# Values of two units in one run: an attention and ELU feed-forward kernel on one core

## The chip, the cores and the metric

The kernel runs on one core of one Trainium2 chip. The metric is the device time of one execution in microseconds (us), the median of three runs. A core has five engines with an instruction stream each: TensorE (PE in the rows, its weight loads PEld), VectorE (DVE), ScalarE (ACT), GpSimd (POOL) and SyncE (SP, which here only issues transfers). They run side by side and wait for each other by semaphores.

## The reference

```python
block, window = (32, 16)
k_sum = k.reshape(B, H, nb, block, D).max(axis=3)
v_sum = v.reshape(B, H, nb, block, D).mean(axis=3)
scores_l = scale * np.matmul(q, k.transpose(0, 1, 3, 2))
mask_l = np.abs(pos[:, None] - pos[None, :]) < window
scores_s = scale * np.einsum('bhsd,bhnd->bhsn', q, k_sum)
scores_s = scores_s + np.log(block)
scores_l_m = np.where(mask_l, scores_l, -1000000000.0)
scores_all = np.concatenate([scores_l_m, scores_s], axis=-1)
...
a = a / (np.sum(a, axis=-1, keepdims=True) + 1e-09)
v_all = np.concatenate([v, v_sum], axis=2)
return np.matmul(a, v_all).astype(np.float32)
...
h = x @ w_in
g = np.where(h > 0.0, h, alpha * (np.exp(np.minimum(h, 0.0)) - 1.0))
return (g @ w_out).astype(np.float32)
```

There are 4 batches, 8 heads, 768 positions and a head dimension of 64. Each query attends to a window of 31 positions and to 24 block summaries. The attention's output, 3072 tokens of 512, goes through a layer of 2048 with ELU and back to 512. All is float32.

## The kernel before

The tokens are cut into six chunks of 512 (`CH`), and a chunk's feed-forward into 16 steps, one for each 128 of the 2048 inner columns. A step is called n, from 0 to 95, with chunk c = n // 16. In each step TensorE does `layer1` (twelve matmuls into `h`, four pieces of x by three products: the float32 values are split into a rounded part and a rest, `xh` and `xl`, `gh` and `gl`, and two parts of each weight) and `layer2` of the step before (twelve matmuls into four accumulators `o`). Between the two, ScalarE takes the exponential of `h`, VectorE makes the ELU of it, ScalarE rounds it to `gh`, and GpSimd subtracts to `gl` (`exp_of`, `elu`, `split`).

The attention that makes the x of the next chunk is spread over the same steps. Its work is in units: a unit is 256 queries (a third of a batch's positions) of one pair of heads, p = 0 to 3. The prologue makes the x of chunk 0; 40 units follow, and eight of them fill a chunk. Unit u has its transposes in step 2u and its values in step 2u + 1, both at the end of the step, in `slot_b`. Its scores come in the even step before, in `slot_a`, between the layers. There too the transfers of the unit after are issued (`load_unit`: `qbd`, `kw`, `vw`, the last two with extra pieces at the edges of a batch). Between scores and transposes, VectorE takes the row maximum (`lowest`), ScalarE the exponentials, GpSimd the normalization. `values` multiplies the transposed weights `pt` with the unit's values `vw[p]` into the bank `o_ps`: eight matmuls by two halves of 64 output partitions, which the profile shows as sixteen. `take_x` brings `o_ps` into x: ScalarE's cast to `xh` (L169), and VectorE's subtraction to `xl` (L170).

Eight banks of PSUM hold four accumulators `o`, two `h`, and two, `a0` and `a1`, that scores, transposes, means and values take in turn after the first chunk (`bank`). There are four `kw` and `vw` tiles, one for each p, so unit u + 4 writes over those of unit u.

For steps 16 to 95 the order on TensorE and SP is the program's; the order on the other engines comes from a scheduler. SP takes its transfers in order, and one that waits holds up all behind it. Early in the chunks before a new batch (steps 24 to 29 and 48 to 53), further transfers `n` bring keys and values for that batch's summaries, and VectorE reduces them (L439).

Of the kernel before, what the change touches and what calls it, by code (L numbers as in the profile page):

```python
# [17 lines left out]
F32 = mybir.dt.float32  # L18
# [8 lines left out]
P = 128  # L27
# [5 lines left out]
UW = 4  # L33
UT = UW * QW
# [4 lines left out]
def attn_elu_ffn(ctx: ExitStack, tc: tile.TileContext, qT, kT, vT, v, w_in, w_out, out):  # L39
# [19 lines left out]
    att = ctx.enter_context(tc.tile_pool(name="att", bufs=2))  # L59
    ffn = ctx.enter_context(tc.tile_pool(name="ffn", bufs=2))  # L60
    wts = ctx.enter_context(tc.tile_pool(name="wts", bufs=1))
    psum = ctx.enter_context(tc.tile_pool(name="psum", bufs=1, space=bass.MemoryType.PSUM))
# [4 lines left out]
    vw = [const.tile([P, UW, P], F32, name=f"vw{p}") for p in range(NP)]  # L67
# [78 lines left out]
    def transposes(sm, tag, bufs=1):  # L146
        t_ps = psum.tile([P, UW, P], F32, tag=tag, name="t_ps", bufs=bufs)
        for t in range(UW):
            nc.tensor.transpose(t_ps[0:KC, t, :], sm[:, t, :], ident)  # L149
        return t_ps  # L150

    def values(v_t, w0, pt, tag):
        o_ps = psum.tile([P, UT], F32, tag=tag, name="o_ps")
        for t in range(UW):
            for h in range(2):
                nc.tensor.matmul(o_ps[h * D:(h + 1) * D, t * QW:(t + 1) * QW],  # L156
                                 v_t[0:KC, w0 + t, h * D:(h + 1) * D], pt[0:KC, t, h * QW:(h + 1) * QW],
                                 start=True, stop=True)
        return o_ps
# [3 lines left out]
    def new_x(c):  # L163
        xs[c] = (att.tile([P, NP, CH], F32R, tag="xh", name="xh"), att.tile([P, NP, CH], F32R, tag="xl", name="xl"))

    def take_x(o_ps, third, p):
        xh, xl = xs[third // 2]
        cols = slice(third % 2 * UT, (third % 2 + 1) * UT)
        nc.scalar.copy(out=xh[:, p, cols], in_=o_ps)  # L169
        nc.vector.tensor_tensor(out=xl[:, p, cols], in0=o_ps, in1=xh[:, p, cols].bitcast(F32), op=ALU.subtract)  # L170
# [17 lines left out]
    def first_units():  # L188
# [118 lines left out]
        def vals(p, th):  # L307
            take_x(values(v_t[p], th * UW, pts[p][:, th], ("a0", "o0", "o1", "o2")[2 * (p % 2) + th]), th, p)
# [82 lines left out]
    units = [(third, p) for third in range(2, NTH * B) for p in range(NP)]  # L391
# [51 lines left out]
    def bank(c):  # L443

        if c == 0:
            return "a0"
        banks["n"] += 1
        return f"a{banks['n'] % 2}"
# [8 lines left out]
    s_of, sm_of, z_of, pt_of = {}, {}, {}, {}  # L457
# [16 lines left out]

    def unit_transposes(u, c):
        t_ps = transposes(sm_of.pop(u), bank(c))
        pt_of[u] = att.tile([P, UW, P], F32, tag="pt", name="pt", bufs=1)
        return lambda: nc.scalar.copy(out=pt_of[u][0:KC], in_=t_ps[0:KC])

    def unit_values(u, c):  # L480
        third, p = units[u]
        if third % 2 == 0 and p == 0:
            new_x(third // 2)
        o_ps = values(vw[p], 0, pt_of.pop(u), bank(c))
        return lambda: take_x(o_ps, third, p)


    gs = {}
# [85 lines left out]
                put_means(b, p, vw[p])  # L574

    def slot_b(n, c):
        u, odd = divmod(n, 2)
        return (unit_values if odd else unit_transposes)(u, c) if u < len(units) else lambda: None

    def begin_next():  # L580

# [8 lines left out]
    with tc.manual_schedule(engines=set(engines.values())):  # L590
# [7 lines left out]
        for n in range(NF):  # L598
            u, odd = divmod(n, 2)
# [30 lines left out]
            if n > 0:  # L630
                layer2(0, n - 1)
            late, this = this, ahead
            evacuate = slot_b(n, 0)
        list(late)
        split(0, NF - 1, e)
# [3 lines left out]
    with tc.manual_schedule(engines={engines["PE"], engines["SP"]}):  # L639
        for n in range(NF, NCH * NF):  # L640
            c, f = divmod(n, NF)
            u, odd = divmod(n, 2)
            h_ps = layer1(c, f)
            e = exp_of(h_ps)
            turn = elu(e, h_ps)
            split(c, f, e)
            slot_a(n, c)
            if not odd and u + 1 < len(units):
                unit_exps(u + 1, unit_low(u + 1))
                unit_norm(u + 1)  # L650
            for b, first in first_of.items():
                p = n - (2 * first - 8)
                if p == 0:
                    new_summaries(b)
                for q, src in ((p, kT), (p - 2, vT)):
                    if 0 <= q < NP:
                        got = load_summary(b, q, src)
                        with tc.issue_after(turn):
                            summary(b, q, src, got)
            layer2(*divmod(n - 1, NF))  # L660
            slot_b(n, c)()
        layer2(NCH - 1, NF - 1)
# [37 lines left out]
```

## Time and profile before

| | |
|---|---|
| median of 3 runs | 657.42 us (657.16 to 658.16) |
| the profiled execution | 658.07 us |
| its span, from the first to the last instruction | 656.3 us |
| TensorE busy | 639.7 us, 97% of the span |
| ScalarE, VectorE, GpSimd busy | 42%, 40%, 37% |
| granted TensorE clock, mean | 0.99 of full speed |

The profile is one execution; its own time lies within the three runs. Busy times of TensorE are of instructions that overlap, so how long something holds TensorE is read as the difference of two starts.

### The profile page before, as it was taken

Reading aid. Unit: us, or ns where it says so; the run is one execution under the profiler, and the core shown is the slowest. Engines: PE = TensorE matmul, PEld = TensorE weight load, DVE = VectorE, ACT = ScalarE, POOL = GpSimd, SP = SyncE. Lnnn points to the kernel's source line nnn. Section 1 sums busy time; section 2 is a strip of 40 time slices with the busy share of each in tenths; the row PEclk is TensorE's granted clock in tenths of the full one; section 3 lists DMA queues with packets and bytes.
Section 4 is the critical chain, followed back from the end, with each engine's and each line's share of the span. In section 5 each row is a group of like instructions: output and inputs, shape, how many; then the busy total and the mean of one; then the engine's idle time right before and its main releaser. Section 6 shows DMA issues by size and latency. Waiting matters only on the chain.

```text
span 656.3 us, 10774 instructions
## 1 busy us (share of the span) xinstructions
PE 639.7 (97%) x3916; PEld 523.8 (80%) x3916; DVE 265.7 (40%) x856; ACT 275.6 (42%) x750; POOL 245.3 (37%) x263
## 2 busy tenths in 40 slices
PE   8859999999999999999999999999999999999997
PEld 7648878888888878888888888888888888888885
DVE  7868887633224533322233543222322231322222
ACT  6757667644334333343344333433443343322222
POOL 5768989843222322232223232322232222222221
PEclk9969999999999999999999999999999999999999
DMA  9999965114122514121112551211321100100001
GB/s 315 208 317 351 308 212 167 33 36 125 32 56 80 151 34 134 36 60 38 32 35 72 171 137 38 70 32 33 97 64 31 32 1 1 64 1 1 0 1 64
DMA packets 86324, 60.24 MB, mean 92 GB/s; under 512 B 46464, under 2 KB 78464, under 8 KB 86272
## 3 DMA queue, kind: packets, MB, share of 16 engines
q1 hardware_dynamic: 82960, 53.66, 29.4%
q10 hardware_dynamic: 3312, 5.90, 2.4%
q8 instruction: 31, 0.51, 0.3%
q14 instruction: 21, 0.17, 0.1%
HBM read 52.46 MB, written 6.29 MB: 90 GB/s over the span
## 4 chain that ended last, share of the span: by engine, by line
PE 94%; DMA 2%; DVE 2%; ACT 1%; POOL 0%; SPq 0%; issue 0%; DVEq 0%
PE h L499 41%; PE o L527 40%; PE s L463 5%; PE o_ps L156 4%; PE t_ps L149 3%; DMA v<-in_v_dram 1%; DMA raw_w<-in_w_in_dram 1%; DMA raw_w<-in_w_out_dram 1%; DVE sm L130 1%; PE idle L227 1%; ACT sm L137 0%; PE s L290 0%; DVE sh L110 0%; DVE cv L113 0%; POOL raw_w L103 0%; DVE ks L276 0%
## 5 line engine op out<-in xcount | busy, mean ns | idle before, releaser
L499 PE MATMUL h<-xh,w 128*128 128x512 f32 x768 | 262.8, 403 | 0.0
L517 POOL TENSOR_TENSOR gl<-e,gh 128x512 fp32r<-128x512 f32 x96 | 123.9, 1290 | 205.3 <-issue 109.6
L527 PE MATMUL o<-w,gh 128*128 128x512 f32 x768 | 196.4, 394 | 0.0
L499 PEld LDWEIGHTS h<-xh,w 128*128 128x128 f32 x768 | 145.3, 189 | 31.2
L527 PEld LDWEIGHTS o<-w,gh 128*128 128x128 f32 x768 | 141.2, 188 | 28.2 <-issue 0.6
L499 PE MATMUL h<-xl,w 128*128 128x512 f32 x384 | 150.9, 393 | 0.0
L509 DVE TENSOR_SCALAR e<-e 128x512 f32<-128x512 f32 x96 | 45.1, 469 | 254.2 <-ACT e L505 254.1
L505 ACT ACTIVATE e<-h 128x512 f32<-128x512 f32 x96 | 57.4, 598 | 210.9 <-PE h L499 210.0
L144 POOL TENSOR_TENSOR sm<-sm,z 128x480 f32<-128x480 f32 x48 | 47.5, 990 | 157.0 <-ACT gh L516 130.9
L527 PE MATMUL o<-w,gl 128*128 128x512 f32 x384 | 105.3, 389 | 0.0
L516 ACT CAST gh<-e 128x512 fp32r<-128x512 f32 x96 | 59.0, 615 | 72.9 <-DVE e L510 71.6
L137 ACT ACTIVATE sm<-sm,mx 128x120 f32<-128x120 f32 x192 | 73.5, 385 | 26.5 <-DVE mx L130 26.5
L527 PEld LDWEIGHTS o<-w,gl 128*128 128x128 f32 x384 | 72.0, 188 | 15.2 <-POOL gl L517 0.2
L499 PEld LDWEIGHTS h<-xl,w 128*128 128x128 f32 x384 | 72.9, 190 | 13.0
L510 DVE SCALAR_TENSOR_TENSOR e<-h,e 128x512 f32<-128x512 f32 x96 | 66.2, 690 | 2.2
L170 DVE TENSOR_TENSOR xl<-o_ps,xh 128x256 fp32r<-128x256 f32 x48 | 20.0, 423 | 61.4 <-ACT xh L169 61.4
L118 POOL TENSOR_TENSOR w<-cv,w 128x512 fp32r<-128x512 f32 x32 | 42.4, 1325 | 6.7 <-ACT w L117 5.8
L463 PEld LDWEIGHTS s<-kw,qbd 128*128 128x128 f32 x320 | 41.8, 191 | 3.7 <-DVE xl L170 0.7
L130 DVE CUSTOM_DVE_ANT_0 sm<-s,mask 128x120 f32<-128x120 f32 x192 | 42.2, 277 | 1.8 <-PE s L463 1.7
L463 PE MATMUL s<-kw,qbd 128*128 128x120 f32 x320 | 41.9, 274 | 0.6 <-DVE xl L170 0.6
L149 PE MATMUL t_ps<-ident,sm 128*120 128x128 f32 x192 | 29.3, 276 | 8.5 <-DVE mx L130 6.8
L137 ACT ACTIVATION_READ_ACCUMULATOR sm<-sm,mx 128x1 f32 x192 | 36.1, 188 | 0.0
(66 smaller groups left out, 361.1 us busy)
## 6 DMA issues: line engine op xcount, KB each, us to landing
raw_w<-in_w_in_dram SPq DMA_DIRECT2D x16, 512.0 KB, 6.3
raw_w<-in_w_out_dram SPq DMA_DIRECT2D x16, 512.0 KB, 6.1
qbd<-in_qT_dram SPq DMA_DIRECT2D x80, 64.0 KB, 2.3
out_dram<-ot ACTq DMA_DIRECT2D x20, 256.0 KB, 3.8
kw<-in_kT_dram SPq DMA_DIRECT2D x28, 144.0 KB, 5.9
vw<-in_v_dram SPq DMA_DIRECT2D x28, 144.0 KB, 2.9
n<-in_kT_dram SPq DMA_DIRECT2D x16, 192.0 KB, 2.5
n<-in_vT_dram SPq DMA_DIRECT2D x16, 192.0 KB, 2.6
```

Of the source, the lines that this page charges most:

```text
L130: nc.vector.tensor_tensor_reduce(out=sm[:, t, :], in0=s_ps[:, t, :], in1=m, scale=-scale, scalar=3.0e38, op0=ALU.add, op1=ALU.min, accum_o ...
L137: nc.scalar.activation(out=sm[:, t, :], in_=sm[:, t, :], func=AF.Exp, bias=mx[:, t, :], scale=-1.0, accum_out=z[:, t, :])
L144: nc.gpsimd.tensor_tensor(out=sm, in0=sm, in1=z.broadcast_to([P, UW, KC]), op=ALU.mult)
L149: nc.tensor.transpose(t_ps[0:KC, t, :], sm[:, t, :], ident)
L463: nc.tensor.matmul(s_of[u][:, t, :], qbd[u % 2][:, t, :], kw[p][:, t, :], start=True, stop=True)
L499: nc.tensor.matmul(h_ps, w[:, a, cols], bb[:, cc, :], start=(k == 0), stop=(k == 3 * NCC - 1))
L505: nc.scalar.activation(out=e, in_=h_ps, func=AF.Exp)
L509: nc.vector.tensor_scalar(out=e, in0=e, scalar1=1.0, scalar2=-1.0, op0=ALU.min, op1=ALU.add)
L510: top = nc.vector.scalar_tensor_tensor(out=e, in0=h_ps, scalar=0.0, in1=e, op0=ALU.max, op1=ALU.add)
L516: nc.scalar.copy(out=gh, in_=e)
L517: nc.gpsimd.tensor_tensor(out=gl, in0=e, in1=gh.bitcast(F32), op=ALU.subtract)
L527: nc.tensor.matmul(o_acc[c][s], a[:, s * P:(s + 1) * P], w[:, bb, :], start=first and f == 0, stop=last and f == NF - 1)
```

## The change

Beyond the first chunk (c > 0), a unit's values no longer stand at the end of each odd step. In steps with n % 4 == 1 nothing stands there. In steps with n % 4 == 3 the values of two units, p and p + 1 of the same third, are written behind each other into the two halves of one bank, and then both are taken into x. The transposed weights have two buffers in place of one, since two units' now wait at a time.

```diff
-    def values(v_t, w0, pt, tag):
-        o_ps = psum.tile([P, UT], F32, tag=tag, name="o_ps")
+    def values(v_t, w0, pt, tag=None, o_ps=None):
+        if o_ps is None:
+            o_ps = psum.tile([P, UT], F32, tag=tag, name="o_ps")
...
         t_ps = transposes(sm_of.pop(u), bank(c))
-        pt_of[u] = att.tile([P, UW, P], F32, tag="pt", name="pt", bufs=1)
+        pt_of[u] = att.tile([P, UW, P], F32, tag="pt", name="pt")
         return lambda: nc.scalar.copy(out=pt_of[u][0:KC], in_=t_ps[0:KC])
...
+    def values_of_two(u, c):
+
+        third, p = units[u]
+        if third % 2 == 0 and p == 0:
+            new_x(third // 2)
+        o_ps = psum.tile([P, 2, UT], F32, tag=bank(c), name="o_ps")
+        for i in range(2):
+            values(vw[p + i], 0, pt_of.pop(u + i), o_ps=o_ps[:, i, :])
+        for i in range(2):
+            take_x(o_ps[:, i, :], third, p + i)
+        return lambda: None
...
     def slot_b(n, c):
+
         u, odd = divmod(n, 2)
-        return (unit_values if odd else unit_transposes)(u, c) if u < len(units) else lambda: None
+        if u >= len(units) or (c > 0 and n % 4 == 1):
+            return lambda: None
+        if not odd:
+            return unit_transposes(u, c)
+        return unit_values(u, c) if c == 0 else values_of_two(u - 1, c)
```

The line numbers of the changed kernel are one to eighteen higher. In its order rows a name like `vw_76` is a tile with its number: `vw_76` to `vw_79` are those of p = 0 to 3.

**TensorE, the ends of steps 17 and 19.** The order at the end of step 17 before:

```order
L527 MATMUL o_1989<-w_0_699,gl 128x512
L527 MATMUL o_1990<-w_0_699,gl 128x512
L527 MATMUL o_1991<-w_0_699,gl 128x512
L527 MATMUL o_1992<-w_0_699,gl 128x512
L156 MATMUL o_ps<-pt,vw_76 64x64 x8
L499 MATMUL h<-xh,w_2_730 128x512
L499 MATMUL h<-xl,w_2_730 128x512
```

and now:

```order
L540 MATMUL o_1989<-w_0_699,gl 128x512
L540 MATMUL o_1990<-w_0_699,gl 128x512
L540 MATMUL o_1991<-w_0_699,gl 128x512
L540 MATMUL o_1992<-w_0_699,gl 128x512
L512 MATMUL h<-xh,w_2_730 128x512
L512 MATMUL h<-xl,w_2_730 128x512
```

Layer 2 is followed by layer 1 of step 18 with nothing between. The end of step 19 now, with the semaphores that each instruction waits for:

```order
L540 MATMUL o_1991<-w_2_850,gl 128x512
L540 MATMUL o_1992<-w_2_850,gl 128x512
L157 MATMUL o_ps<-pt,vw_76 64x64 [waits DVE_49]
L157 MATMUL o_ps<-pt,vw_76 64x64 x7
L157 MATMUL o_ps<-pt,vw_77 64x64 [waits DMAHW2_49,Activation_49]
L157 MATMUL o_ps<-pt,vw_77 64x64 x7
L512 MATMUL h<-xh,w_4_882 128x512 [waits DVE_49]
```

Unit 8's values stand behind unit 9's transposes now, directly ahead of unit 9's values. For comparison, the last values of the prologue, which the change does not touch; five units' worth of them stand behind each other (`values` is called once for each third), and these are the last four:

```order
L156 MATMUL o_ps<-pt_509,v_90 64x64 [waits DMAHW1_49]
L156 MATMUL o_ps<-pt_509,v_90 64x64
L156 MATMUL o_ps<-pt_509,v_90 64x64 [waits DMAHW0_49]
L156 MATMUL o_ps<-pt_509,v_90 64x64 x5
L156 MATMUL o_ps<-pt_509,v_90 64x64 [waits DVE_49]
L156 MATMUL o_ps<-pt_509,v_90 64x64 x7
L156 MATMUL o_ps<-pt_549,v_91 64x64 [waits DMAHW3_49,DVE_49,Pool_49]
L156 MATMUL o_ps<-pt_549,v_91 64x64
L156 MATMUL o_ps<-pt_549,v_91 64x64 [waits DMAHW2_49]
L156 MATMUL o_ps<-pt_549,v_91 64x64 x5
L156 MATMUL o_ps<-pt_549,v_91 64x64 [waits DVE_49]
L156 MATMUL o_ps<-pt_549,v_91 64x64 x7
```

There, too, instructions in the middle of a row of values wait for transfers and engines.

**ScalarE, the casts of units 8 and 9.** Before, around the end of step 19:

```order
L505 ACTIVATE e<-h 128x512 [waits PE_49,Pool_49]
L516 CAST gh<-e 128x512 [waits DVE_49]
L169 CAST xh<-o_ps 128x256 [waits PE_49]
L505 ACTIVATE e<-h 128x512 [waits PE_49,Pool_49]
L137 ACTIVATE sm,z<-sm,mx 128x120 [waits DVE_49] x4
```

and now:

```order
L518 ACTIVATE e<-h 128x512 [waits PE_49,Pool_49]
L529 CAST gh<-e 128x512 [waits DVE_49]
L170 CAST xh<-o_ps 128x256 [waits PE_49]
L170 CAST xh<-o_ps 128x256 [waits DVE_49]
L518 ACTIVATE e<-h 128x512 [waits PE_49,Pool_49]
L137 ACTIVATE sm,z<-sm,mx 128x120 [waits DVE_49] x4
```

The cast of unit 8 has moved from step 17 to here, and the second cast waits for VectorE. On VectorE the two subtractions have moved in the same way.

**SP, the transfers of unit 14, issued for step 24.** Before:

```order
L398 DMA qbd_70<-in_qT_dram 64x4x64 [waits DMAHW3_49,PE_49]
L398 DMA qbd_70<-in_qT_dram 64x4x64 [waits DMAHW4_49]
L404 DMA kw_74<-in_kT_dram 128x3x96 [waits DMAHW5_49]
L408 DMA vw_78<-in_v_dram 96x3x128 [waits DMAHW6_49]
L416 DMA kw_74<-in_kT_dram 128x80 [waits DMAHW7_49]
L417 DMA vw_78<-in_v_dram 80x128 [waits DMAHW0_49]
L430 DMA n<-in_kT_dram 128x384 [waits DVE_49,DMAHW1_49,Activation_49,Pool_49]
```

and now:

```order
L399 DMA qbd_70<-in_qT_dram 64x4x64 [waits DMAHW3_49,PE_49]
L399 DMA qbd_70<-in_qT_dram 64x4x64 [waits DMAHW4_49]
L405 DMA kw_74<-in_kT_dram 128x3x96 [waits DMAHW5_49]
L409 DMA vw_78<-in_v_dram 96x3x128 [waits DMAHW6_49,PE_49]
L417 DMA kw_74<-in_kT_dram 128x80 [waits DMAHW7_49]
L418 DMA vw_78<-in_v_dram 80x128 [waits DMAHW0_49,PE_49]
L431 DMA n<-in_kT_dram 128x384 [waits DVE_49,DMAHW1_49,Activation_49,Pool_49]
```

The order of SP's transfers is the same all through the program. What is new is that the `vw` transfers of units with p = 0 and 2 wait for TensorE; those with p = 1 and 3 do not.

## Rows read from the trace of the kernel before

**Rows 1.** The page, part 1: busy us, share of the span, instructions.

```profile
PE 639.7 (97%) x3916; PEld 523.8 (80%) x3916; DVE 265.7 (40%) x856; ACT 275.6 (42%) x750; POOL 245.3 (37%) x263
```

**Rows 2.** The page, part 4: the chain that ended last, by engine.

```profile
PE 94%; DMA 2%; DVE 2%; ACT 1%; POOL 0%; SPq 0%; issue 0%; DVEq 0%
```

**Rows 3.** What TensorE waited for from 31 us on: total, times, longest.

```profile
PE t_ps L149 <- DVE mx L130: 6.8, 1, 6.8
```

**Rows 4.** Timeline of TensorE, step 84, without attention: start, us, what.

```profile
583.13 0.39 PE L499 MATMUL h<-xh,w 128*128 128x512 f32 x1
...
585.86 1.98 PE L527 MATMUL o<-w,gh 128*128 128x512 f32 x8
...
588.58 0.39 PE L499 MATMUL h<-xh,w 128*128 128x512 f32 x1
```

**Rows 5.** Timeline of TensorE, steps 41 and 42.

```profile
306.52 0.48 PE L499 MATMUL h<-xh,w 128*128 128x512 f32 x1
...
309.36 1.98 PE L527 MATMUL o<-w,gh 128*128 128x512 f32 x8
...
312.17 0.69 PE L156 MATMUL o_ps<-pt,vw 120*64 120x64 f32 x16
312.79 0.50 PE L499 MATMUL h<-xh,w 128*128 128x512 f32 x1
...
315.64 1.05 PE L463 MATMUL s<-kw,qbd 128*128 128x120 f32 x8
316.45 2.07 PE L527 MATMUL o<-w,gh 128*128 128x512 f32 x8
318.36 1.07 PE L527 MATMUL o<-w,gl 128*128 128x512 f32 x4
```

**Rows 6.** Timeline of TensorE, values in the prologue.

```profile
24.01 0.69 PE L156 MATMUL o_ps<-pt,v 120*64 120x64 f32 x16 [0.58 <-POOL v L174]
...
25.67 2.55 PE L156 MATMUL o_ps<-pt,v 120*64 120x64 f32 x80
```

**Rows 7.** Windows: busy us by engine, granted clock (PEclk), DMA share, GB/s.

```profile
25.60:28.30 2.70, 2.62 (x82) 2.42 (x80) 1.32 (x3) 1.88 (x5) 2.02 (x3) 1.00 0.77 230
306.52:319.62 13.10, 13.10 (x80) 10.77 (x78) 3.73 (x15) 4.92 (x14) 3.53 (x4) 1.00 0.17 40
```

**Rows 8.** Timeline of ScalarE, VectorE and TensorE at the start of step 32.

```profile
247.45 0.37 ACT L169 CAST xh<-o_ps 128x256 fp32r<-128x256 f32 x1 [1.43 <-PE o_ps L156]
250.45 0.60 ACT L505 ACTIVATE e<-h 128x512 f32<-128x512 f32 x1 [2.62 <-PE h L499]
...
247.86 0.42 DVE L170 TENSOR_TENSOR xl<-o_ps,xh 128x256 fp32r<-128x256 f32 x1 [2.49 <-ACT xh L169]
...
249.06 0.39 PE L499 MATMUL h<-xl,w 128*128 128x512 f32 x1
...
249.74 0.39 PE L499 MATMUL h<-xl,w 128*128 128x512 f32 x1
```

**Rows 9.** Timeline of ScalarE and GpSimd, from h to gl of step 41.

```profile
309.62 0.60 ACT L505 ACTIVATE e<-h 128x512 f32<-128x512 f32 x1 [2.17 <-PE h L499]
311.44 0.62 ACT L516 CAST gh<-e 128x512 fp32r<-128x512 f32 x1 [1.22 <-DVE e L510]
...
312.19 1.28 POOL L517 TENSOR_TENSOR gl<-e,gh 128x512 fp32r<-128x512 f32 x1 [3.65 <-issue]
```

**Rows 10.** SP, TensorE, VectorE near step 24; last row: all transfers n.

```profile
187.29 0.48 SPq L408 DMA_DIRECT2D vw<-in_v_dram  x1
...
188.93 12.32 SPq L430 DMA_DIRECT2D n<-in_kT_dram  x4
...
194.39 0.50 PE L499 MATMUL h<-xh,w 128*128 128x512 f32 x1
...
199.88 1.00 DVE L439 TENSOR_REDUCE ks<-n 128x12 f32<-128x384 f32 x2
...
DMA to landing us min/median/max: 2.3/2.5/2.7
```

## The prediction

> **What bounds the kernel now.** I read the page first. TensorE is busy for 639.7 us, 97% of the span, no other engine for more than 42% of the span [rows 1], and the chain that ended last lies on TensorE for 94% [rows 2]. Because a busy TensorE need not be one that runs at its pace, I then read what it waits for: from 31 us to the end the waits view has a single wait of TensorE, 6.8 us in the first chunk's first step [rows 3], which the change does not touch. So from step 16 on nothing feeds TensorE late, and a time there can only come from what TensorE itself executes and from how its instructions follow each other. That is read from starts in the timeline, not from busy sums, since matmuls overlap.
>
> A step without attention is the yardstick: layer 1 starts at 583.13, layer 2 at 585.86, the next step's layer 1 at 588.58 [rows 4]. Each layer's twelve matmuls take 2.72 us, a step 5.44. Against that stands step 41, an odd step with values, and the layer 1 of step 42 after it [rows 5]. Layer 2 runs from 309.36 to the first values matmul at 312.17, 2.81 us instead of 2.72. The values stand from 312.17 to the next layer 1 at 312.79, 0.62. That layer 1 runs to the scores at 315.64, 2.85 instead of 2.72. So one run of values costs 0.09 + 0.62 + 0.13 = 0.84 us of TensorE, of which some 0.2 is a slower entry and a slower first matmul after it. The same pattern stands in all 32 odd steps from 17 to 79. (The layer 1 of step 41, 2.84, pays 0.12 for the transposes ahead of it. That stays.)
>
> **What the change takes away and adds on TensorE.** Units 8 to 39 come after the first chunk: 16 pairs. Each pair had two runs, and now has one, in the steps with n % 4 == 3. As the order rows show, the steps with n % 4 == 1 go from layer 2's last matmul straight to layer 1. The instruction count is the same: sixteen profiled matmuls for a unit.
>
> Taken away for each pair: one run, 0.84 us.
>
> Added: the second unit's sixteen matmuls, directly behind the first's. The prologue has exactly this. A single unit there is 16 matmuls in 0.69 us, and five units back to back are 80 in 2.55 [rows 6], so each further unit costs (2.55 - 0.69)/4 = 0.465 us, 29 ns a matmul, 58 ns for a pair of halves, at the same granted clock of 1.00 as the steps have [rows 7]. Those five write four banks in turn, read three pt tiles, and carry semaphore waits in the middle of the run, as their order rows show; at 0.465 a unit, waits that are long met cost nothing. The new run has the same kind of wait at its second unit.
>
> The bounds of this term: 0.465 is also the pace within one run, and nothing in the rows is faster, so it is the lower end. The upper end is 0.62, a whole run with its start and its end again, if the other half of the bank or the wait breaks the stream [rows 5]. I take 0.465, since [rows 6] shows the same instructions back to back.
>
> What the trace shows of the pace is 29 ns a matmul [rows 6]. The Trainium skill's "TensorE: Matmul & The Clock Gate" (section "Wait — 56ns, not 53.3ns?") speaks against the change: with hardware decode off it gives about 62 ns per matmul as the bound for small matmuls. By that figure sixteen more would be an estimated 0.99 us, more than the 0.84 taken away, and the sum would be some 2.4 us slower. The trace does not agree that this bound holds here.
>
> Sum: (0.84 - 0.465) x 16 = 0.375 x 16 = **6.0 us**; with the upper bound (0.84 - 0.62) x 16 = 3.5 us.
>
> **What moves beside TensorE, and what hides it.**
>
> *Taking the values out of the bank.* Both units share a bank, so no cast starts before the whole run is done, and by the order rows of ScalarE the second cast waits for VectorE, that is for the first subtraction: cast, subtraction, cast, subtraction, one after the other. Behind the waiting cast on ScalarE stands the exp of the next h. It matters first where the next step reads that x, the four chunk edges (into steps 32, 48, 64 and 80). At step 32 today the cast runs from 247.45 for 0.37 us and the subtraction from 247.86 for 0.42 [rows 8], 0.87 from a cast's start to the next free start with the 0.04 between them. So the first xl is ready at 248.28 and the second at 249.15. Layer 1 takes pair 2's xl in its eighth matmul at 249.06 and pair 3's in its eleventh at 249.74 [rows 8]: margins of 0.78 and 0.59 us, and exp waits until 250.45 anyway. Nothing is on the path. If the cover were gone, each us late would cost a us at only four places. In steps 27 and 51 a subtraction stands behind a summary reduce that waits for its transfer; that holds the pair up by the reduce, and only there.
>
> *A shorter way to layer 2.* With its values gone, step 41 gives its h less time until layer 2 needs gh and gl. Today exp starts at 309.62, gh is done at 312.06 and gl at 313.47 [rows 9]. They are needed at 316.45 and 318.36 [rows 5], and after the change 0.84 earlier, 315.61 and 317.52. Margins of 3.5 and 4.0 us remain. The steps without attention have even less time between and do not wait [rows 3, 4].
>
> *The values' transfers.* By the order rows the vw loads of even units (vw_76, vw_78) now also wait for TensorE: the unit that used the tile before has its values two steps later, at the end of step n - 1 for the load issued by step n. Behind that wait, in SP's order, stand the rest of the load and in steps 24 and 48 the first summary transfers, which VectorE takes in its own order. For step 24 the vw load was issued at 187.29, the first n at 188.93, 1.64 later [rows 10]. Now vw goes when the values of step 23 end, no later than the start of step 24 at 194.39. So the first n goes at 196.0 and lands 2.5 later, at 198.5, its second half some half a us behind; VectorE reduces the first at 199.88 [rows 10]. Margin about 1.3 us; were it gone, VectorE would be late by that much, with the 3.5 us of the paragraph above before TensorE feels it. What else is behind the wait, the edge pieces of kw and vw of a unit, is first needed by the scores two steps later, over 12 us by the steps' lengths [rows 5]. SP's next qbd load waits for scores of the coming step anyway.
>
> *The rest.* The second pt buffer only removes a wait. Nothing of the prologue, the first chunk or the last sixteen steps changes.
>
> The profiled execution took 658.07 us, 0.65 above the median of the runs, 657.42. Its sum gives 658.07 - 6.0 = 652.1. I carry the difference over to the median: **651.4 us**, 0.9% faster. A change below 0.2%, 1.3 us, cannot be told from none here.
>
> **The rivals.**
>
> *The second unit pays for a run of its own* (0.62 for 0.465). For it: the run now crosses to another half of one bank and to a tile that ScalarE wrote a step ago, which the prologue's runs do not have in this form. Against it: the unbroken 80 matmuls [rows 6]. 657.42 - 3.5 = 653.9.
>
> *The time comes back as a wait*: a chunk edge, VectorE in the twelve summary steps, or a late transfer takes what the steps gave. Against it are the margins of 0.59, 1.3 and 3.5 us; to eat 6 us at four edges, 1.5 at each, the last xl would have to be 2.1 us later than worked out. 657.4.
>
> *The halves fall apart, slower than before*: a unit's two matmuls of 64 columns run beside each other today, 58 ns for both. If, in the run of two, each took 58 ns by itself, the second unit would cost 16 x 0.058 = 0.93 against 0.84 taken away: 16 x 0.09 = 1.4 us slower, 658.9. It decides from 0.84/16 = 52 ns a matmul on. Against it: 29 ns over 80 matmuls [rows 6]. The figure of the Trainium skill's page on TensorE, told above, would do its harm at this place.
>
> **How the numbers follow.** My forecast has 0.83, the second unit with a run of its own 0.08, the wait that comes back 0.05, slower 0.04. The likeliest alone would be 650.7 to 652.2: 0.02 us of reading error on a pair's 0.375 is 0.3 us, and the three runs shown lie within 1.0. The range takes in the second case: 650.6 to 653.9, and leaves out the two last. Faster by over 0.2%: 0.83 + 0.08 = 0.91; same 0.05; slower 0.04.
>
> **What would show it.** In the changed kernel's timeline: steps with n % 4 == 1 of 6.27 - 0.09 - 0.62 = 5.56 us (6.27 from 306.52 to 312.79 in [rows 5]); the layer 1 behind them at 2.72; a run of 32 values matmuls that holds from its start to the next layer 1 for 0.62 + 0.465 = 1.08; the step around it 6.73. No wait of TensorE after the first chunk. Cast, subtraction, cast, subtraction at each pair, and SP waiting for TensorE ahead of vw of even units. I would be wrong if the run of two shows a hole in its middle, if layer 1 at steps 32, 48, 64 or 80 shows idle time ahead of an xl matmul, or if layer 2 of an odd step starts late.

## The result: 0.9% faster, and the profile after

The changed kernel takes 652.14 us (median of four runs, 650.75 to 653.99), the kernel before in the same set 657.79 (657.16 to 658.33): a ratio of 0.9908 [0.9891, 0.9925]. Put on the 657.42 from which the prediction started, that is 651.4 us. That this meets the forecast to the tenth is luck: two further sets, below, give 652.5 and 650.6 on the same base. The two medians lie 5.65 us apart; the sum gave 6.0. Either is several times what this measurement can tell from no change, 1.3 us.

**The steps.** First the timeline of the changed kernel on TensorE, from step 41 to the scores of step 44 (start, us, what). Its first rows stand against [rows 5].

```profile
306.03 0.48 PE L512 MATMUL h<-xh,w 128*128 128x512 f32 x1
...
308.87 1.98 PE L540 MATMUL o<-w,gh 128*128 128x512 f32 x8
...
311.59 0.39 PE L512 MATMUL h<-xh,w 128*128 128x512 f32 x1
...
314.31 1.05 PE L464 MATMUL s<-kw,qbd 128*128 128x120 f32 x8
...
318.29 0.47 PE L512 MATMUL h<-xh,w 128*128 128x512 f32 x1
...
321.12 1.98 PE L540 MATMUL o<-w,gh 128*128 128x512 f32 x8
...
323.93 1.15 PE L157 MATMUL o_ps<-pt,vw 120*64 120x64 f32 x32
325.01 0.50 PE L512 MATMUL h<-xh,w 128*128 128x512 f32 x1
...
327.86 1.05 PE L464 MATMUL s<-kw,qbd 128*128 128x120 f32 x8
```

Step 41 is 5.56 us (306.03 to 311.59) and has layer 2 followed by layer 1 after 2.72, as in the step without attention [rows 4]. The layer 1 of step 42 runs 2.72 to its scores. In step 43 the run of 32 values starts 2.81 after layer 2 and holds TensorE for 1.08, and the layer 1 behind it has 2.85. So the entry (0.09) and the exit (0.13) stand once for a pair, and step 43 is 6.72. The run is one row: it has no hole.

**All 64 steps between the first and the last chunk.** The windows view (start and end of the window, its us; then busy us of TensorE, its weight loads, VectorE, ScalarE, GpSimd; granted clock, DMA share, GB/s), each from the first matmul of step 16 to that of step 80. The kernel before:

```profile
143.12:561.24 418.12, 418.12 (x2439) 342.57 (x2435) 139.56 (x512) 160.35 (x450) 114.27 (x105) 1.00 0.23 63
```

The changed kernel:

```profile
144.83:557.15 412.32, 412.32 (x2439) 342.47 (x2436) 139.54 (x511) 159.74 (x449) 114.63 (x105) 1.00 0.23 64
```

The same number of matmuls at the same granted clock takes 5.80 us less; the term of the sum for these steps was 6.0. The busy time of TensorE shows none of it, since in both it fills the window: only the starts do. In the changed kernel step 16 starts 1.7 us later, although ahead of it only the second `pt` buffer is new. The waits view of TensorE (what it waited for; total, times, longest) names the place, the wait of [rows 3], which was 6.8 there. The changed kernel, from 30 us on:

```profile
PE t_ps L149 <- POOL raw_w L103: 7.8, 1, 7.8
```

So the profiled execution drew 1.0 us more of that wait (the other 0.7 us lie ahead of step 0, whose layer 1 starts at 30.42 here and at 29.70 before), and its span, 652.2, is 4.1 us below that of before though its steps save 5.8. From 30 us on there is no other wait of TensorE.

### The profile page after: what moved, and what is told of

Its sections match the earlier page's. It is cut to its first block, busy times and chain, and to the rows that moved or that the text cites. A ratio compares the mean times of both kernels' runs of the same rounds, so it can differ in the third digit from the quotient of the medians.

```text
span 652.2 us, 10758 instructions
## 1 busy us (share of the span) xinstructions
PE 634.6 (97%) x3916; PEld 524.4 (80%) x3916; DVE 264.8 (41%) x856; ACT 275.5 (42%) x750; POOL 245.4 (38%) x263
## 4 chain that ended last, share of the span: by engine, by line
PE 95%; DMA 2%; POOL 1%; DVE 1%; SPq 1%; issue 0%; ACT 0%; POOLq 0%
PE h L512 41%; PE o L540 40%; PE s L464 5%; PE o_ps L157 3%; PE t_ps L149 3%; DMA raw_w<-in_w_in_dram 2%; PE s L291 2%; PE idle L228 1%; POOL sm L144 0%; POOL raw_w L103 0%; POOL w L118 0%; SPq L399 0%; PE vsps L454 0%; DVE sh L110 0%; DVE cv L113 0%
```

## The experiments

**The change twice again.** Both times the changed kernel as it is.

> The changed kernel once more, unaltered. In its first profile the 64 steps with units (16 to 79) take 5.80 us less than before, but step 16 starts at 144.83 instead of 143.12. If that later start is chance of the transfers in the prologue, a second profile shows the same 412.3 us from step 16 to step 80 (to 0.1 us) and another start of step 16, and the times stay 5 to 7 us below those of before. If the change itself makes the prologue later, step 16 starts again near 144.8, 1.5 us or more after that of before.

> The changed kernel a third time, beside the run above: 412.1 to 412.3 us from step 16 to step 80, and a start of step 16 anywhere between 142 and 145, as the prologue falls.

Measured: 652.75 us (652.43 to 654.03; 0.9925 [0.9911, 0.9938]) and 651.91 (651.29 to 653.26; 0.9897 [0.9881, 0.9914]). The steps 16 to 80 of the second take 412.05 us (143.01 to 555.06); the window of the first:

```profile
143.89:555.95 412.06, 412.06 (x2440) 342.58 (x2436) 138.65 (x511) 159.62 (x449) 114.61 (x105) 1.00 0.23 64
```

418.12 - 412.06 = 6.06 us, twice: the term is 6.0 within 0.1. The start of step 16 moves from profile to profile (143.01, 143.89, 144.83), so the whole time of one execution tells less of this change than the window does. From here on the window is the measure, and the ratio stands beside it.

**The second buffer alone.** The rival here is that the second `pt` buffer, which frees the transposes of a wait, gave some of the gain.

```diff
-        pt_of[u] = att.tile([P, UW, P], F32, tag="pt", name="pt", bufs=1)
+        pt_of[u] = att.tile([P, UW, P], F32, tag="pt", name="pt")
```

> The kernel before with the second pt buffer alone. My theory (each run of values that stands apart costs 0.375 us beside its pace, and nothing else was won) gives no change: 657.4, within 1.3 us, and 418.1 us from step 16 to step 80. The rival, that the second buffer frees ScalarE's copy and by that the steps, gives a part of the 6 us: steps shorter than 6.26 and 6.83. If the second buffer is what makes the prologue later, step 16 starts 1.5 us later than in the profile of before.

Measured: 658.08 us, 1.0002 [0.9993, 1.0011]. Its window:

```profile
143.01:561.08 418.07, 418.07 (x2439) 342.54 (x2435) 140.11 (x512) 160.10 (x450) 113.95 (x105) 1.00 0.23 63
```

418.07 against 418.12: the buffer is worth nothing.

**Both units in the same step, in two runs.** This takes from the change only that the two units stand behind each other. Steps with n % 4 == 1 are empty as in the change and the transfers wait as there, but the first unit's values stand between layer 1 and layer 2 of the other odd step, the second's behind its layer 2, each with its own bank.

```diff
-        return unit_values(u, c) if c == 0 else values_of_two(u - 1, c)
+        return unit_values(u, c)
...
+            if n % 4 == 3 and u < len(units):
+                unit_values(u - 1, c)()
             layer2(*divmod(n - 1, NF))
```

> Both units' values in the steps with n % 4 == 3 as in the change, the other odd steps empty, all transfers and waits as in the change, but the first unit's run stands ahead of layer 2 and the second's behind it, each with a bank of its own. If runs count (my theory), nothing is won: two runs of 0.84 as before, 657.4 within 1.3 us, the full steps 7.1 us and the empty ones 5.56. If it counts that odd steps are empty, that transfers wait longer or that both units come in one step, the 6 us stay: 651.5 to 652.

Measured: 657.91 us, 0.9995 [0.9986, 1.0004]. TensorE in step 43 of this kernel:

```profile
319.92 0.47 PE L512 MATMUL h<-xh,w 128*128 128x512 f32 x1
...
322.84 0.69 PE L157 MATMUL o_ps<-pt,vw 120*64 120x64 f32 x16
323.46 2.11 PE L540 MATMUL o<-w,gh 128*128 128x512 f32 x8
...
326.40 0.69 PE L157 MATMUL o_ps<-pt,vw 120*64 120x64 f32 x16
327.02 0.50 PE L512 MATMUL h<-xh,w 128*128 128x512 f32 x1
```

Each of the two runs stands for 0.62 us, and the layer 2 between them, from 323.46 to 326.40, takes 2.94 = 2.72 + 0.13 + 0.09: it pays the exit of one run and the entry of the next. The step is 7.10. With the empty step of 5.56 a pair takes 12.66, against 5.56 + 6.72 = 12.28 in the change: 0.38 for each pair, the predicted 0.375. Its window:

```profile
144.54:562.18 417.64, 417.64 (x2439) 342.75 (x2435) 135.94 (x512) 159.90 (x450) 114.94 (x105) 1.00 0.23 63
```

So fewer steps with values, the new waits of the transfers and the second buffer give 0.5 us at most, and the run that is saved gives the rest. Even these 0.5 us are not theirs: 0.46 stand in steps 31 and 55, which take 7.45 us where 7.68 would follow (7.10, and the 0.58 that a batch's means add to steps 31 and 55 in the kernel before). There the means, which split the array too, stand directly ahead of the first run. This is the experiment that shows the cause.

**A bank for each unit.** The prediction's second bound let the other half of the bank, or the wait, break the run in two. Here the run of two writes two banks, and so the second cast need not wait for the first subtraction.

```diff
-        return unit_values(u, c) if c == 0 else values_of_two(u - 1, c)
+        if c == 0:
+            return unit_values(u, c)
+        first, second = unit_values(u - 1, c), unit_values(u, c)
+        first()
+        second()
+        return lambda: None
```

> The change with a bank for each of the two units, the runs still directly behind each other. If only the run counts, the same as the change: 6 us below before, 1.08 us from the run's start to the next layer 1, and casts that no longer wait for VectorE. If the one bank is what makes the second unit cheap, the run is longer, up to 0.62 + 0.62 = 1.24, and the time up to 2.5 us above that of the change; if the one bank holds something up (its casts take turns), this is faster than the change by what the edges of the chunks lose, which the trace of the change puts at under 0.3 us.

Measured: 652.15 us, 0.9909 [0.9895, 0.9922]. Its timeline at the end of step 43, TensorE and ScalarE:

```profile
321.09 1.15 PE L157 MATMUL o_ps<-pt,vw 120*64 120x64 f32 x32
322.17 0.50 PE L512 MATMUL h<-xh,w 128*128 128x512 f32 x1
...
321.82 0.84 ACT L170 CAST xh<-o_ps 128x256 fp32r<-128x256 f32 x2 [0.84 <-PE o_ps L157]
```

The run is 1.08 again, and the casts, now back to back and from before the run's end, change nothing in the time. One bank or two is the same here, and cast, subtraction, cast, subtraction has its cover.

**Values over the whole array.** What is it in a run that costs more than its matmuls? Here, in the kernel before, the values beyond the first chunk are four matmuls with 128 output partitions instead of eight with 64. Half of each product is not used; two casts and two subtractions of 64 partitions take the useful blocks out. (Each of these matmuls shows as two records in the profile, in either form.)

```diff
...
-        o_ps = values(vw[p], 0, pt_of.pop(u), bank(c))
-        return lambda: take_x(o_ps, third, p)
...
+        for t in range(UW):
+            nc.tensor.matmul(o_ps[:, t, :], vw[p][0:KC, t, :], pt[0:KC, t, :], start=True, stop=True)
+        return lambda: take_halves(o_ps, third, p)
```

> The kernel before, with one run in every odd step, but beyond the first chunk a unit's values as four matmuls over all 128 output partitions (both heads' values by both heads' weights; only the two diagonal blocks are taken into x, by two casts and two subtractions of 64 partitions). The array is then never split in two halves after the first chunk. If the 0.375 us of a run belong to the change between whole and split array, this run costs what the scores cost, 8 records of 0.112 and about 0.1 of exit: 1.0 in place of 0.84, 5 us slower than before, 663, with a layer 2 of 2.72 ahead of it. If every run apart pays 0.375 whatever its shape, it costs 0.9 + 0.375 = 1.27, 13.8 us slower, 672.

Measured: 660.33 us, 1.004 [1.0027, 1.0053]. TensorE in step 41 and the layer 1 behind it:

```profile
311.22 1.98 PE L548 MATMUL o<-w,gh 128*128 128x512 f32 x8
...
313.94 1.05 PE L505 MATMUL o_ps<-pt,vw 120*128 120x128 f32 x8
314.75 0.48 PE L520 MATMUL h<-xh,w 128*128 128x512 f32 x1
...
317.57 0.38 PE L463 MATMUL s<-kw,qbd 128*128 128x120 f32 x2
```

Layer 2 runs 2.72 to the values: the entry of 0.09 is gone when the values do not split the array. The run stands for 0.81, like the eight records of the scores [rows 5: 315.64 to 316.45]. The layer 1 behind it has 2.82, 0.10 more than its own. One run is 0.81 + 0.10 = 0.91 instead of 0.84, a little slower. Now set this against the run's own pace, as the 0.465 of split values is a pace: the eight records start 0.111 apart (313.94 to 314.72 for seven), so eight are 0.89. The run costs its pace and 0.02. The 0.10 in the layer 1 behind it is not an exit like that of split values, but mostly the rest of the last record's own time, since layer 1 starts 0.03 after that record. My expectation was too high because it counted this twice; the other expectation there is refuted. Of the 0.375 that a run costs beside its pace, all but some 0.02 is gone when the array is not split.

The rows show where it goes. In the layers the weights of a matmul are loaded (PEld) 0.22 us ahead of it, beside the matmul before: at 311.37 for the one at 311.59 in the changed kernel. The loads around the run of step 43 in the changed kernel, and its last two records:

```profile
323.93 1.01 PEld L157 LDWEIGHTS o_ps<-pt,vw 120*64 120x64 f32 x32 [0.35 <-issue]
325.01 0.19 PEld L512 LDWEIGHTS h<-xh,w 128*128 128x128 f32 x1
...
324.85 0.23 PE L157 MATMUL o_ps<-pt,vw 120*64 120x64 f32 x2
```

and those of the values over the whole array, with their last record:

```profile
313.72 1.09 PEld L505 LDWEIGHTS o_ps<-pt,vw 120*128 120x128 f32 x8
314.72 0.19 PEld L520 LDWEIGHTS h<-xh,w 128*128 128x128 f32 x1
...
314.72 0.28 PE L505 MATMUL o_ps<-pt,vw 120*128 120x128 f32 x1
```

Over the whole array the first load goes 0.22 ahead of its matmul (313.94), and layer 1's first load goes with the last record. Into and out of the run of split values no load runs ahead: its first comes after 0.35 of idle time and with the run itself, and layer 1's with layer 1, 0.16 after the last two records. So the 0.62 - 0.465 = 0.155 at the run's own ends is some 0.10 behind its last two records (0.16, where the pace is 0.058) and 0.05 behind its first two (the next follow 0.107 later). The means of a batch, which split the array in four, have the same 0.09 and 0.35 ahead of them: in step 31 of the kernel before, they start at 243.41, 0.32 after layer 1's last matmul, where the pace is 0.23. The kernel here changes the width of the matmuls together with the split; that the split is what costs rests on these rows.

**The scores ahead of the run of two.** If the entry and the exit belong to all short matmuls together, the scores directly ahead of the values would pay them once for both. The scores of steps with n % 4 == 0 move to the end of the step before.

```diff
+            if n % 4 != 0 or n <= NF:
+                unit_scores(u + 1, c)
...
+        if u + 2 < len(units):
+            unit_scores(u + 2, c)
+        return values_of_two(u - 1, c)
```

> The change, with the scores of the steps with n % 4 == 0 moved to the end of the step before, directly ahead of the run of two (15 of 16 places). Today scores leave layer 2 behind them 0.09 late, and the run of values makes the layer 2 ahead of it 0.09 longer. If what is paid is the change from the long matmuls of the layers to short ones and back, one of the two is saved at each place: 15 x 0.09 = 1.4 us below the change, 650.7. If it is the change between whole and split array, the values behind the scores pay the same entry as behind layer 2: at most the scores' own exit is won, and with a dearer entry nothing, 652.1.

Measured: 653.47 us, 0.9934 [0.9921, 0.9946], above the changed kernel. TensorE in step 43:

```profile
320.73 1.98 PE L540 MATMUL o<-w,gh 128*128 128x512 f32 x8
...
323.45 1.05 PE L464 MATMUL s<-kw,qbd 128*128 128x120 f32 x8
324.43 1.15 PE L157 MATMUL o_ps<-pt,vw 120*64 120x64 f32 x32
325.51 0.50 PE L512 MATMUL h<-xh,w 128*128 128x512 f32 x1
```

Layer 2 runs 2.72 to the scores, but the scores hold 0.98 to the values, where they hold 0.81 to a layer 2. Of these 0.17 more, 0.08 is the rest of the last record's own time, which a layer 2 behind scores has in its first matmul: eight records at 0.111 are 0.89, and 0.09 is left. So the values' entry is paid behind short matmuls too, at the same 0.09, and the run is 1.08 as ever. Its window:

```profile
144.14:557.29 413.15, 413.15 (x2439) 344.39 (x2435) 139.57 (x511) 159.81 (x449) 114.73 (x105) 1.00 0.23 63
```

That is 1.1 us more than 412.06. Most of it stands at the chunk edges, where the cover that the prediction spoke of is gone: the scores come earlier, so ScalarE's exponentials of them stand ahead of the casts, and the layer 1 pauses for `xl`. ScalarE and TensorE at step 32:

```profile
248.61 0.35 ACT L170 CAST xh<-o_ps 128x256 fp32r<-128x256 f32 x1
249.46 0.37 ACT L170 CAST xh<-o_ps 128x256 fp32r<-128x256 f32 x1 [0.50 <-DVE xl L171]
...
247.72 0.50 PE L512 MATMUL h<-xh,w 128*128 128x512 f32 x1
...
250.91 0.62 PE L540 MATMUL o<-w,gh 128*128 128x512 f32 x2
```

That layer 1 takes 3.19 us (247.72 to 250.91), as do those of steps 48 and 64; away from the edges the layer 1 behind a run has 2.88 in this kernel. Three times 0.31 is 0.9 of the 1.1. The rest of the steps is even: 7.61 + 5.95 = 13.56 us for steps 43 and 44, where the change has 6.72 + 6.83 = 13.55.

**The first chunk too.** The change leaves the first chunk's eight units alone. With four more pairs the time would be four times 0.375 lower. As with single units there, a pair of the first chunk is taken into x in the next step; that part of the edit is not shown.

```diff
...
-        if u >= len(units) or (c > 0 and n % 4 == 1):
+        if u >= len(units) or n % 4 == 1:
...
-        return unit_values(u, c) if c == 0 else values_of_two(u - 1, c)
+        return values_of_two(u - 1, c)
```

> The change, with the values in pairs in the first chunk as well (steps 3, 7, 11 and 15). If only the number of runs counts, four runs fewer: 4 x 0.375 = 1.5 us below the change, 650.6 to 651. The rival: in the first chunk SP also brings the weights, and vw transfers that wait for TensorE hold these up, so TensorE waits for weights and the time is that of the change or some us above it.

Measured: 652.75 us, 0.9922 [0.9908, 0.9937]: nothing over the change. The steps without values and the run of two have the predicted lengths, but step 8 is 7.10 instead of 6.83 and step 16 is 6.45 instead of 5.70. At step 16 the last pair is late for its reader. TensorE and ScalarE there:

```profile
140.79 1.04 PE L513 MATMUL h<-xh,w 128*128 128x512 f32 x2
...
140.91 0.37 ACT L170 CAST xh<-o_ps 128x256 fp32r<-128x256 f32 x1 [2.26 <-PE o_ps L157]
141.77 0.37 ACT L170 CAST xh<-o_ps 128x256 fp32r<-128x256 f32 x1 [0.49 <-DVE xl L171]
```

The layer 1 that reads `xh` of the pair stops until the casts are through, the second a subtraction after the first. That is the rival "the time comes back as a wait" at the one edge where the prediction's margins do not hold: five of this layer 1's twelve matmuls stand ahead of the values there, so the pair is read 5 x 0.227 = 1.1 us earlier than at the other edges. So of 4 x 0.375 = 1.5 us that the four pairs should give, step 8 takes 0.27 back and step 16 takes 0.75; some 0.5 is left, too little to tell.

**The first chunk but for its last pair.** The same, with units 6 and 7 singly in steps 13 and 15.

```diff
...
+        if u < len(units) and n in (13, 15):
+            return unit_values(u, c)
```

> The change, with pairs in the first chunk too, but at its end (steps 13 and 15) single runs as before, since the run of two there held up the x of step 16 by 0.75 us. Three runs fewer: 3 x 0.375 = 1.1 us, less 0.27 that the run of two in step 7 lost at the x or weights of step 8: from step 2 to step 17 some 98.2 us, where the change takes 99.05. Of the time, 0.8 us below the change, no more than the prologue moves from run to run. If steps of the first chunk are held by weights, 99.05 or above.

Measured: 651.05 us (649.85 to 651.84), 0.9876 [0.9856, 0.9896]; the changed kernel beside it 651.91. From step 2 to step 17 it takes 98.91 us (49.23 to 148.14), the changed kernel beside it 99.04 (49.66 to 148.70).

It saves 0.13 there, not the 0.8 that I expected, because I had overlooked that the first run taken away stands in step 1, ahead of the window (0.09 + 0.62 = 0.71 us, worked out). Three pairs less what step 8 gives back, 3 x 0.375 - 0.28 = 0.85 us, is what the sum comes to, and the two medians lie 0.86 apart. The intervals of the two ratios overlap, so by time alone it is not shown to be faster. In step 8, too, the second of the two subtractions is late; TensorE and VectorE in it:

```profile
92.06 1.12 PE L464 MATMUL s<-kw,qbd 128*128 128x120 f32 x8
...
90.07 0.69 DVE L113 SCALAR_TENSOR_TENSOR cv<-raw_w,sh 128x512 uint32<-128x512 uint32 x1
90.68 0.42 DVE L171 TENSOR_TENSOR xl<-o_ps,xh 128x256 fp32r<-128x256 f32 x1
91.53 0.42 DVE L171 TENSOR_TENSOR xl<-o_ps,xh 128x256 fp32r<-128x256 f32 x1 [0.44 <-ACT xh L170]
```

The scores start at 92.06, just after the second subtraction ends at 91.95, and the first of the two stands behind an operation of the weights' conversion (`cv`), which the first chunk has. In the first chunk `bank` gives one bank to all, so these scores write where the pair still stood. That they wait for this subtraction is read from these times; no run takes it away.

A run of four units was not tried.

## Why the prediction was right

**The price of a run, 0.84.** Right in each part, and at another place too: entry, 0.62 and exit stand between layer 1 and layer 2 in the kernel with two runs in one step.

**The second unit at 0.465.** Right: the run of two is 1.08 us in the change and with a bank for each unit. The rival in which it pays its own run needed 1.24. The figure of 62 ns per matmul from the Trainium skill's "TensorE: Matmul & The Clock Gate" (section "Wait — 56ns, not 53.3ns?") is not what this run pays: its second sixteen records add 1.08 - 0.62 = 0.46 us, 29 ns each. But the prediction counted sixteen where the order rows have eight matmuls, two records each, and for each of these eight it is 58 ns. Counted so, the page's figure gives an estimated 0.50 us for the second unit and a gain of 5.5, and does not speak against the change. No run here shows which count the figure is for. The halves did not fall apart.

**The sum, 6.0.** The steps gave 5.80, 6.06 and 6.07 in three profiles of the change. The 0.2 that the first lacks is in two steps, 17 and 65, which took 5.62 and 5.73 instead of 5.56. The timeline of the changed kernel at step 65, TensorE and VectorE:

```profile
464.30 2.13 PE L540 MATMUL o<-w,gh 128*128 128x512 f32 x8
...
464.95 0.69 DVE L561 COPY ot<-o 128x512 f32<-128x512 f32 x1 [3.40 <-DMA out_dram<-ot]
```

The accumulators of the chunk before are still being copied out by VectorE, which had waited for an output transfer, when the shorter step brings the first layer 2 of the new chunk. The prediction had looked at what feeds layer 2, not at what empties its accumulators. It is a loss of 0.17 us in one step, and in the two other profiles of the change it is not there; in that of the last experiment step 65 takes 5.94, a loss of 0.38.

**The taking out at the chunk edges.** Right to the hundredth. ScalarE, VectorE and TensorE of the changed kernel at step 32, against [rows 8]:

```profile
247.71 0.37 ACT L170 CAST xh<-o_ps 128x256 fp32r<-128x256 f32 x1 [1.90 <-PE o_ps L157]
248.57 0.37 ACT L170 CAST xh<-o_ps 128x256 fp32r<-128x256 f32 x1 [0.49 <-DVE xl L171]
...
248.11 0.42 DVE L171 TENSOR_TENSOR xl<-o_ps,xh 128x256 fp32r<-128x256 f32 x1 [2.96 <-ACT xh L170]
248.98 0.42 DVE L171 TENSOR_TENSOR xl<-o_ps,xh 128x256 fp32r<-128x256 f32 x1 [0.44 <-ACT xh L170]
...
249.31 0.39 PE L512 MATMUL h<-xl,w 128*128 128x512 f32 x1
...
249.99 0.39 PE L512 MATMUL h<-xl,w 128*128 128x512 f32 x1
```

The parts of x are there at 248.53 and 249.40 and are read at 249.31 and 249.99: margins of 0.78 and 0.59 us, the ones forecast. The kernel with the first chunk in pairs and the one with the scores ahead show what is lost where they are missing.

**The transfers.** Right. SP at step 24 of the changed kernel, and VectorE's first reduce:

```profile
194.92 0.33 SPq L409 DMA_DIRECT2D vw<-in_v_dram  x1
196.41 0.81 SPq L431 DMA_DIRECT2D n<-in_kT_dram  x2
...
200.89 1.00 DVE L440 TENSOR_REDUCE ks<-n 128x12 f32<-128x384 f32 x2
```

The `vw` load goes 0.5 us before the step starts (195.39), the first `n` 1.49 after it. With the median landing of 2.5 it is there at 198.9, 2.0 ahead of the reduce; the forecast was 1.3. The waits cost nothing that the window shows.

**The way to layer 2.** Right: in step 41 `gl` is issued at 311.70 for 1.28 us and read at 317.02, as worked out a margin of 4.0. Step by step nothing of the forecast failed, but for the small loss at step 65, which it did not have. What the median lacks of 6.0, 0.35, is within what the wait in the prologue moves from one execution to the next: its longest row is 6.1 us in the profile with a bank for each unit, 7.8 in that of the change, and 9.2 in that with two runs in one step, whose program is the same up to there.

**What the price is made of.** The prediction took the 0.375 from starts and did not say what makes it. The kernel with values over the whole array does: it is the change between whole and split array, and no weights are loaded ahead across it. On this the Trainium skill's "TensorEngine Tiling (Array Packing)" (section "Key Properties") says that a change of the tiling mode drains TensorE. The idle 0.35 of the loads, and the 0.09 that stands behind layer 2 and behind the scores alike, agree with it; the page gives no price. Open is whether the width of the matmuls has a part in the price, since no run splits the array and keeps them wide.

## What to carry to other kernels

When TensorE is always fed, look for runs of short matmuls between long ones and read, from starts, what the neighbours lose as well as what the run holds: here 0.375 of 0.84 us belonged to the run and not to its work, and putting two runs together saved just that. Set a run with both its neighbours against its own pace: what looks like a price behind it can be the rest of its last matmul, as with the scores. The runs that paid here are those that split the array. Before a run is moved later, work out when its last result is read at each edge; margins of 0.6 us held, and where other work stood on the engine that takes the results out, the whole gain was gone. Compare the stretch that was changed by its own window, since a wait elsewhere can move the total by more than the change does.

## What was not expected of the hardware

The values over the whole array have twice the products but half the records, and cost only 0.07 us a run more (0.91 against 0.84): they pay their pace and next to nothing beside it. And a run of split matmuls pays the same 0.09 us of entry behind short matmuls over the whole array as behind long ones: short work ahead does not share its entry, unless it splits the array as well, like the means.
